# Attention and two FFNs in one kernel: dependent products of a unit further apart, other engines' steps later, M1's block sums moved

## Chip, cores, metric

One core of a Trainium2 chip. The metric is the device time of one execution in microseconds (us). The kernel before takes 1079.6 us, the median of three runs (1079.17 to 1079.61).

## What is computed

```python
qn = q / (norm(q, axis=1) + 1e-6); kn = k / (norm(k, axis=1) + 1e-6)   # norms over the 6016 tokens
a = softmax(kn.T @ qn / tau)                                           # 256 x 256
x = v @ a                                                              # 6016 x 256
h = x @ w_in;  g = h * clip(h + 3, 0, 6) / 6;  x = g @ w_out           # FFN 1: 256 -> 2048 -> 256
h = x @ w_in2; g = max(h, 0) ** 2;             x = g @ w_out2          # FFN 2
```

All inputs are float32; the weights arrive as float64 words.

## The kernel before

**Numbers.** Each float32 matrix is split into a high part `hi` (a cast to fp32r, on ScalarE) and a rest `lo` (the subtraction x - hi). `passes` (lines 298 to 306) makes one product of three TensorE instructions: hi with hi, the left rest with hi, hi with the right rest.

**Stages.** While q and k are loaded, TensorE sums the scores. The softmax is folded into the weights: M1 = a w_in1, in four blocks of 512 columns (blocks 0 to 3, `c4`; line 440 on). The tokens go in six pairs (`WIDTHS`: two column blocks of 512 each, the last pair 448) through layer 1 (j = 0) and then layer 2 (j = 1). The first pair of layer 1 runs as 32 plain steps (lines 834 to 857), because the weights are still being made: a step has `first` (product, relu, multiply, split) and, two steps later, `second`, the products with w_out1. At steps 6, 14 and 22 it makes the next block of M1. Its casts of w_in1 and w_out1 from float64 are spread over the steps by `plan`.

**A Strassen unit.** All other pairs run in units of 256 columns of w_in (`strassen`, lines 702 to 786), eight a pair, 15 places each (`SLOTS`); a place is one product. Seven products make the four blocks of h from sums of blocks of x and of M1. Bank y takes B11, T2, T1 and B22 one on top of the other; ScalarE copies y after the first three as `sa`, `su`, `se`, and the next product into y waits for the copy. Bank x takes B21, bank q takes T3 and later T4. Then h11 = x + sa, h22 = q + se before T4 is added, h21 = q + su after it, and h12 is y itself. T4 waits for the sum h22. Each block goes through relu (ScalarE; layer 1, and h12 in both), multiply (VectorE), `hi` (ScalarE) and `lo` (VectorE) to a group: two products with w_out into `acc`. The eight group products of a unit fill the places that its successor's seven products leave.

**Order.** Every engine works through its instructions in program order. `at(place, go)` notes a step with its place, and `run` emits the steps sorted by place, so the numbers alone set the order on each engine. `PLACE` has the products, `chain` the five steps of each block (add, relu, multiply, hi, lo), `prepare` a pair's input sums and splits (GpSimd makes sums and rests; they start 52.5 places ahead), `times` the nine steps that turn a piece of layer 2's weights into parts while layer 1 runs (the 6th sums on GpSimd, 7th parts on ScalarE, 8th rests on GpSimd, 9th the store).

**M1's sums.** `m1_keep` copies a block of M1 to two buffers, which all blocks share with the operands T1 and T4; `m1_sums` makes four sums on GpSimd; `m1_parts` casts them (ScalarE, 1024 elements) and takes the rest (GpSimd). Only Strassen units use them.

```python
        m1_sum_at = {1: 0}
        m1_sum_at |= {8 * c4 - M1_LEAD + 2: c4 for c4 in range(1, 4)}
...
            if a in m1_sum_at:
                c4 = m1_sum_at[a]
                sums_of[c4] = m1_sums(c4)
            if a - 3 in m1_sum_at:
```

So the sums of blocks 0 to 3 stand at steps 1, 8, 16 and 24, the parts at steps 4, 11, 19 and 27.

## Time and profile before

| | us | |
|---|---|---|
| profiled execution | 1079.58 | its span 1077.8 |
| median of three runs | 1079.6 | 1079.17 to 1079.61 |
| ScalarE busy | 672.5 | 62% of the span |
| GpSimd busy | 256.5 | 24% |
| mean granted TensorE clock | 0.995 | of full speed |

In the rows PE is TensorE, PEld its weight loads, DVE VectorE, ACT ScalarE, POOL GpSimd. A line number is that of the kernel above; a helper's line (L120, the subtraction in `split`) stands for all its callers, so the names tell which. "[1.71 <-ACT wi1h L118]" means: the engine was idle for 1.71 us, and what ended last before it went on was ScalarE's writing of wi1h. PEclk is the granted clock as a share of full speed.

### The profile page before, as it was taken

The numbers are of one execution on the slowest core, as the hardware profiler recorded it, in microseconds if no ns is written. First come the engines' busy times: TensorE is split into PE (matmuls) and PEld (weight loads), VectorE is DVE, ScalarE is ACT, GpSimd is POOL, SyncE is SP. The second block draws the span as 40 slices with busy tenths as digits, with TensorE's granted clock in tenths as the row PEclk, the third lists the DMA queues.
The fourth block names the chain that finished last, engine by engine and source line by source line (L and its number), as shares of the span: only waits on it lengthen the run. The fifth ranks groups of instructions, "written<-read, shape, count | busy, mean of one in ns | idle before, by whom it ended". The sixth has DMA issues, their size and how long they took to land.

```text
span 1077.8 us, 13113 instructions
## 1 busy us (share of the span) xinstructions
PE 1049.4 (97%) x4630; PEld 865.8 (80%) x4630; DVE 866.6 (80%) x1283; ACT 672.5 (62%) x1196; POOL 256.5 (24%) x215
## 2 busy tenths in 40 slices
PE   9989899999989998999999999999999999999998
PEld 8867677877868786788998888888888888888997
DVE  7798977799888888887778878778778778778766
ACT  6677667768767777777767545545445445445443
POOL 0022351154244245234114004104104105004000
PEclk9999999999999999999999999999999999999999
DMA  9721302213212330420344200200200200200100
GB/s 352 301 62 36 98 1 79 93 39 132 93 61 75 110 106 25 143 77 20 127 166 187 102 1 1 78 1 1 79 1 1 79 0 1 74 1 1 40 1 35
DMA packets 25938, 77.66 MB, mean 72 GB/s; under 512 B 2832, under 2 KB 4880, under 8 KB 25872
## 3 DMA queue, kind: packets, MB, share of 16 engines
q1 hardware_dynamic: 25872, 76.82, 19.9%
q8 instruction: 36, 0.59, 0.2%
q14 instruction: 30, 0.25, 0.1%
HBM read 52.95 MB, written 23.86 MB: 71 GB/s over the span
## 4 chain that ended last, share of the span: by engine, by line
PE 75%; DVE 12%; ACT 6%; issue 5%; POOL 2%; DMA 1%; SPq 0%; DVEq 0%; ACTq 0%; POOLq 0%
PE acc L304 13%; PE acc L306 13%; PE acc L305 13%; PE y L304 7%; PE y L306 6%; PE y L305 6%; PE q L304 3%; PE s L294 3%; PE q L306 3%; PE q L305 3%; DVE gs L120 3%; DVE g L744 3%; DVE h L730 2%; PE x L304 2%; PE x L306 2%
## 5 line engine op out<-in xcount | busy, mean ns | idle before, releaser
L120 DVE TENSOR_TENSOR gs<-g,gs 128x512 fp32r<-128x512 f32 (+1 forms) x384 | 280.5, 748 | 65.1 <-ACT gs L753 58.8
L305 PE MATMUL acc<-gs,wo 128*128 128x512 f32 (+1 forms) x768 | 297.0, 387 | 1.1 <-DVE wo L120 1.1
L306 PE MATMUL acc<-gs,wo 128*128 128x512 f32 (+1 forms) x768 | 297.3, 387 | 0.7 <-DVE gs L120 0.7
L304 PE MATMUL acc<-gs,wo 128*128 128x512 f32 (+1 forms) x768 | 297.4, 387 | 0.1
L753 ACT CAST gs<-g 128x512 fp32r<-128x512 f32 (+1 forms) x352 | 214.3, 611 | 116.0 <-DVE g L749 59.3
L306 PEld LDWEIGHTS acc<-gs,wo 128*128 128x128 f32 x768 | 144.7, 188 | 30.6 <-DVE gs L120 3.3
L305 PEld LDWEIGHTS acc<-gs,wo 128*128 128x128 f32 x768 | 144.8, 189 | 28.7 <-DVE wo L120 1.4
L304 PEld LDWEIGHTS acc<-gs,wo 128*128 128x128 f32 x768 | 144.9, 189 | 28.4 <-ACT gs L118 0.8
L685 POOL TENSOR_TENSOR x<-raw,x 128x512 fp32r<-128x512 f32 (+1 forms) x55 | 78.1, 1428 | 324.9 <-ACT x L681 323.7
L749 DVE SCALAR_TENSOR_TENSOR g<-h 128x512 f32<-128x512 f32 (+1 forms) x144 | 123.8, 860 | 3.1
L744 DVE SCALAR_TENSOR_TENSOR g<-r,h 128x512 f32<-128x512 f32 (+1 forms) x120 | 99.8, 832 | 28.7 <-ACT r L736 24.9
L736 ACT ACTIVATE r<-h,three 128x512 f32<-128x512 f32 (+1 forms) x120 | 85.6, 713 | 33.5 <-DVE h L730 32.8
L730 DVE TENSOR_TENSOR h<-q,su 128x512 f32<-128x512 f32 (+1 forms) x88 | 59.6, 677 | 40.2 <-PE q L306 40.0
L730 DVE TENSOR_TENSOR h<-q,se 128x512 f32<-128x512 f32 (+1 forms) x88 | 59.5, 676 | 33.0 <-ACT se L726 32.9
L738 ACT ACTIVATE r<-y 128x512 f32<-128x512 f32 (+1 forms) x48 | 28.3, 590 | 84.4 <-PE y L306 84.4
L726 ACT COPY se<-y 128x512 f32<-128x512 f32 (+1 forms) x88 | 50.6, 575 | 35.2 <-PE y L306 35.1
L726 ACT COPY sa<-y 128x512 f32<-128x512 f32 (+1 forms) x88 | 50.2, 570 | 32.5 <-PE y L306 31.9
L726 ACT COPY su<-y 128x512 f32<-128x512 f32 (+1 forms) x88 | 50.0, 569 | 31.2 <-PE y L306 31.2
L730 DVE TENSOR_TENSOR h<-x,sa 128x512 f32<-128x512 f32 (+1 forms) x88 | 59.4, 675 | 8.4 <-PE x L306 7.3
L670 POOL TENSOR_TENSOR t<-raw 128x512 f32<-128x512 f32 (+1 forms) x11 | 17.2, 1566 | 110.4 <-DMA raw<-x2d 110.4
L294 PE MATMUL s<-qk 128*128 128x256 f32 x188 | 42.5, 386 | 0.6 <-DMA qk<-in_qk 0.6
L294 PEld LDWEIGHTS s<-qk 128*128 128x128 f32 x188 | 36.0, 194 | 6.2 <-DMA qk<-in_qk 1.4
(238 smaller groups left out, 1878.2 us busy)
## 6 DMA issues: line engine op xcount, KB each, us to landing
qk<-in_qk SPq DMA_DIRECT2D x23, 512.0 KB, 7.3
wo<-in_w_out SPq DMA_DIRECT2D x16, 512.0 KB, 4.5
wi<-in_w_in SPq DMA_DIRECT2D x10, 512.0 KB, 4.3
x2d<-o SPq DMA_DIRECT2D x20, 256.0 KB, 2.5
raw<-x2d SPq DMA_DIRECT2D x10, 512.0 KB, 5.3
out<-o SPq DMA_DIRECT2D x20, 256.0 KB, 2.3
raw<-in_vt SPq DMA_DIRECT2D x8, 512.0 KB, 5.8
wo2d<-wo2s SPq DMA_DIRECT2D x8, 512.0 KB, 2.9
```

The costliest lines, as they stand in the source:

```text
L120: (rest or nc.vector).tensor_tensor(out=lo, in0=x, in1=f32(hi), op=ALU.subtract)
L294: nc.tensor.matmul(s_ps[i], lhsT=x[:, C + i * P:C + (i + 1) * P], rhs=x[:, :C], start=(t == 0), stop=(t == NT - 1))
L304: nc.tensor.matmul(ps, lhsT=ah, rhs=bh, start=first, stop=False, skip_group_check=more)
L305: nc.tensor.matmul(ps, lhsT=al, rhs=bh, start=False, stop=False, skip_group_check=more)
L306: nc.tensor.matmul(ps, lhsT=ah, rhs=bl, start=False, stop=last, skip_group_check=more)
L685: nc.gpsimd.tensor_tensor(out=l, in0=ts[r], in1=f32(h), op=ALU.subtract)
L726: nc.scalar.copy(s[tag], s["y"])
L730: nc.vector.tensor_tensor(out=s[which], in0=s[ps], in1=s[tag], op=ALU.add)
L736: nc.scalar.activation(s["r" + which], h, AF.Relu, bias=three)
L744: nc.vector.scalar_tensor_tensor(out=g, in0=s["r" + which], scalar=6.0, in1=h, op0=ALU.min, op1=ALU.mult)
L749: nc.vector.scalar_tensor_tensor(out=g, in0=h, scalar=0.0, in1=r, op0=ALU.max, op1=ALU.mult)
L753: nc.scalar.copy(gs[which][0], s["g" + which])
```

## The change

- Products: `PLACE` puts T2, T3, T1, B22 and T4 at 5, 7, 10, 14 and 16 instead of 4, 6, 8, 12 and 13. T4 now runs at place 1 of the next unit. The groups stand at the other places, as pairs, in the order 11, 22, 12, 21 (before 11, 22, 21, 12).
- The steps of `chain` and the copies su and se stand later.
- M1's sums move to steps 10, 17, 25 and 28, its parts to 14, 20, 27 and 30, each part as two halves. The copies go to a spare tile of each block.
- The parts, rests and store of layer 2's w_in move from 27.4, 28.5 and 36 to 36, 38 and 48.
- The split of the first pair's last step is placed among the first Strassen unit's steps, and the casts of T1 and T4 for the second pair one and two places earlier.

```diff
-PLACE = {0: B11, 2: B21, 4: T2, 6: T3, 8: T1, 12: B22, 13: T4}
+PLACE = {0: B11, 2: B21, 5: T2, 7: T3, 10: T1, 14: B22, 16: T4}
+GROUP = {"11": (3, 4), "22": (6, 8), "12": (9, 11), "21": (12, 13)}
...
-                m32[k] = ops.tile([P, 2 * WMAX], F32, tag=f"op{(T1, T4)[k]}", name=f"m32_{c4}_{k}")[:, :512]
-                nc.scalar.activation(m32[k], mps.pop((c4, k)), AF.Copy, scale=rsum[k])
+                if k == 0:
+                    m32[c4] = spare(2 * c4 + 1, f"m32_{c4}").rearrange("p (k f) -> p k f", k=KC)
+                nc.scalar.activation(m32[c4][:, k, :], mps.pop((c4, k)), AF.Copy, scale=rsum[k])
...
-            hi, lo = (t[:, :, S1:, :] for t in wa1[c4])
-            nc.scalar.copy(hi, st)
-            nc.gpsimd.tensor_tensor(out=lo, in0=st, in1=f32(hi), op=ALU.subtract)
+            for u in range(2):
+                hi, lo = (t[:, u, S1:, :] for t in wa1[c4])
+                nc.scalar.copy(hi, st[:, u, :, :])
+                nc.gpsimd.tensor_tensor(out=lo, in0=st[:, u, :, :], in1=f32(hi), op=ALU.subtract)
...
-            split(*gs, g)
+            if at_step == len(steps) - 1:
+                at(1.6, lambda: split(*gs, g, 0))
+                at(3.0, lambda: split(*gs, g, 1))
+            else:
+                split(*gs, g)
...
-                        after = {T1: -16, T4: -11, T3: 0.3, B22: 3.0}[r]
+                        after = {T1: -17, T4: -13, T3: 0.3, B22: 3.0}[r]
...
-            at(at0 + 5.3, lambda: copy_out("su"))
-            at(at0 + 9.3, lambda: copy_out("se"))
+            at(at0 + 6.3, lambda: copy_out("su"))
+            at(at0 + 11.3, lambda: copy_out("se"))
             chain = {
-                "11": (3.3, 4.6, 6.0, 7.4, 8.9), "22": (10.4, 11.7, 13.1, 14.6, 16.0),
-                "12": (None, 13.4, 15.5, 17.5, 18.8), "21": (14.4, 15.8, 17.3, 19.0, 20.4),
+                "11": (3.6, 7.2, 9.6, 12.2, 13.8), "22": (12.6, 13.9, 15.2, 16.5, 17.8),
+                "12": (None, 15.4, 17.0, 18.5, 20.0), "21": (17.4, 18.8, 20.4, 22.0, 23.4),
             }
...
-                times = (8.7, 9.5, 17.3, 19.4, 22.4, 25, 27.4, 28.5, 36)
+                times = (8.7, 9.5, 17.3, 19.4, 22.4, 25, 36, 38, 48)
...
-        m1_sum_at = {1: 0}
-        m1_sum_at |= {8 * c4 - M1_LEAD + 2: c4 for c4 in range(1, 4)}
+        sums_at, parts_at = {10: 0, 17: 1, 25: 2, 28: 3}, {14: 0, 20: 1, 27: 2, 30: 3}
```

ScalarE in a unit of the second pair, before and after. The names are the block's number, then layer, pair and unit: r11 is relu, gs11 the cast of g11, w32 a piece of layer 2's weights; `0_1_3` is layer 1, pair 1, unit 3.

```order
L736 ACTIVATE r210_1_2_1785<-h210_1_2_1775,three_90 128x512
L726 COPY sa0_1_3_1791<-y0_1_3_1779 128x512
L753 CAST gs120_1_2_1800<-g120_1_2_1783 128x512
L753 CAST gs210_1_2_1808<-g210_1_2_1797 128x512
L736 ACTIVATE r110_1_3_1814<-h110_1_3_1805,three_90 128x512
L726 COPY su0_1_3_1819<-y0_1_3_1779 128x512
L753 CAST gs110_1_3_1831<-g110_1_3_1826 128x512
L224 COPY w32_0_1833<-tawi2_0_1739 128x512
L726 COPY se0_1_3_1842<-y0_1_3_1779 128x512
```

The same part of the program as it is now:

```order
L744 ACTIVATE r120_1_2_1778<-y0_1_2_1675,three_90 128x512
L734 COPY sa0_1_3_1783<-y0_1_3_1772 128x512
L761 CAST gs220_1_2_1785<-g220_1_2_1776 128x512
L761 CAST gs120_1_2_1800<-g120_1_2_1787 128x512
L744 ACTIVATE r210_1_2_1804<-h210_1_2_1794,three_90 128x512
L734 COPY su0_1_3_1819<-y0_1_3_1772 128x512
L761 CAST gs210_1_2_1821<-g210_1_2_1814 128x512
L744 ACTIVATE r110_1_3_1827<-h110_1_3_1802,three_90 128x512
L226 COPY w32_0_1829<-tawi2_0_1736 128x512
L734 COPY se0_1_3_1852<-y0_1_3_1772 128x512
L761 CAST gs110_1_3_1857<-g110_1_3_1838 128x512
```

Before, sa stands behind the relu of block 21, su behind that of block 11, and se behind the cast of block 11. Now sa stands behind the relu of 12, su ahead of the relu of 11, and se ahead of the cast of 11.

GpSimd in the first pair, up to the second pair's first sums, before (st are block sums, wa1 the parts; t, x the second pair's sums and rests):

```order
L484 TENSOR_TENSOR wa1_1l_771<-st1_849,wa1_1h_770 128x2x512
L207 TENSOR_TENSOR st2_1099<-m32_2_0_1034,m32_2_1_1036 128x2x128
L208 TENSOR_TENSOR st2_1099<-st2_1099,m32_2_0_1034 128x2x128
L209 TENSOR_TENSOR st2_1099<-m32_2_0_1034 128x2x128
L210 TENSOR_TENSOR st2_1099<-m32_2_1_1036,st2_1099 128x2x128
L484 TENSOR_TENSOR wa1_2l_1019<-st2_1099,wa1_2h_1018 128x2x512
L670 TENSOR_TENSOR t0_1_0_1244<-raw0_1_0_1159 128x512
L671 TENSOR_TENSOR t0_1_1_1245<-raw0_1_1_1160,t0_1_0_1244 128x512
```

And now, up to the same two sums of the second pair:

```order
L488 TENSOR_TENSOR wa1_0l_531<-st0_895,wa1_0h_530 128x512 x2
L209 TENSOR_TENSOR st1_1120<-m32_1_778 128x2x128
L210 TENSOR_TENSOR st1_1120<-st1_1120,m32_1_778 128x2x128
L211 TENSOR_TENSOR st1_1120<-m32_1_778 128x2x128
L212 TENSOR_TENSOR st1_1120<-m32_1_778,st1_1120 128x2x128
L488 TENSOR_TENSOR wa1_1l_763<-st1_1120,wa1_1h_762 128x512 x2
L678 TENSOR_TENSOR t0_1_0_1238<-raw0_1_0_1151 128x512
L679 TENSOR_TENSOR t0_1_1_1239<-raw0_1_1_1152,t0_1_0_1238 128x512
```

Three blocks are done ahead of the second pair's sums before, and two now; the other two come behind them.

## Rows read from the trace of the kernel before

**Rows 1.** The page, part 1: engine, busy us (share of the span), instructions.

```profile
PE 1049.4 (97%) x4630; PEld 865.8 (80%) x4630; DVE 866.6 (80%) x1283; ACT 672.5 (62%) x1196; POOL 256.5 (24%) x215
```

**Rows 2.** Windows: stretch in us, its length, then busy us (instructions) by engine, clock, DMA.

```profile
core 0: us, PE busy (x) PEld busy (x) DVE busy (x) ACT busy (x) POOL busy (x), PEclk, DMA share, GB/s
50.40:175.00 124.60, 112.67 (x463) 85.24 (x463) 105.07 (x165) 88.90 (x153) 40.45 (x31) 0.99 0.16 52
175.00:455.00 280.00, 269.33 (x1145) 214.47 (x1144) 239.08 (x344) 209.21 (x373) 96.84 (x89) 0.99 0.24 85
600.00:1000.00 400.00, 400.00 (x1762) 330.20 (x1762) 314.53 (x439) 201.44 (x356) 79.42 (x55) 1.00 0.07 24
```

**Rows 3.** TensorE's waits, whole span: line, what ended them, us in total, times, longest.

```profile
PE mp L304 <- ACT wi1h L118: 6.6, 3, 3.5
PE y L304 <- ACT su L726: 5.8, 8, 2.6
PE y L304 <- ACT se L726: 2.5, 3, 0.9
PE q L304 <- DVE h L730: 2.2, 2, 1.9
PE y L304 <- ACT sa L726: 1.3, 3, 0.8
PE mp L306 <- DVE wi1l L120: 1.2, 1, 1.2
...
PE acc L305 <- DVE wo L120: 1.1, 1, 1.1
```

**Rows 4.** Windows, columns as in rows 2: three stretches of layer 1.

```profile
320.60:331.00 10.40, 8.81 (x32) 7.11 (x33) 8.08 (x10) 7.49 (x14) 6.42 (x5) 0.84 0.38 139
140.00:160.00 20.00, 20.00 (x88) 16.17 (x87) 14.81 (x20) 13.32 (x23) 13.46 (x10) 1.00 0.00 1
128.00:140.00 12.00, 8.49 (x30) 6.34 (x29) 10.92 (x14) 6.86 (x13) 5.52 (x3) 0.86 0.00 0
```

**Rows 5.** Line 120, VectorE's subtractions: times, then ns min/median/max.

```profile
L120 DVE TENSOR_TENSOR gs<-g,gs x384: 609/684/1789, 60.9 to 1071.1; 128x512 fp32r<-128x512 f32 x160, 128x448 fp32r<-128x448 f32 x32
...
L120 DVE TENSOR_TENSOR wo<-tawo,wo x8: 684/693/1206, 62.0 to 151.3; 128x512 fp32r<-128x512 f32 x8
```

**Rows 6.** Timeline around M1 block 1: start, length in us, engine, line ... [idle before it].

```profile
74.72 1.03 ACT L483 CAST wa_0h<-st 128x1024 fp32r<-128x1024 f32 x1
...
75.83 2.37 POOL L484 TENSOR_TENSOR wa_0l<-st,wa_0h 128x1024 fp32r<-128x1024 f32 x1 [13.15 <-ACT wa_0h L483]
...
76.89 0.50 PE L304 MATMUL mp<-wi1h,eth 128*128 128x512 f32 x1 [1.71 <-ACT wi1h L118]
76.97 1.77 DVE L120 TENSOR_TENSOR wi1l<-tawi,wi1h 128x512 fp32r<-128x512 f32 x1
...
78.80 0.50 PE L306 MATMUL mp<-wi1l,eth 128*128 128x512 f32 x1 [1.17 <-DVE wi1l L120]
```

**Rows 7.** Timeline around M1 block 3.

```profile
128.97 1.82 DVE L157 SCALAR_TENSOR_TENSOR tawi<-tbwi,tawi 128x512 int32<-128x512 int32 x1
...
132.40 1.74 DVE L162 CUSTOM_DVE_ANT_0 tawi<-tawi,tywi 128x1024 uint16<-128x1024 uint16 x1
...
134.84 0.55 PE L304 MATMUL mp<-wi1h,eth 128*128 128x512 f32 x1 [3.51 <-ACT wi1h L118]
```

**Rows 8.** Timeline, a unit of the second pair.

```profile
222.06 1.78 DVE L744 SCALAR_TENSOR_TENSOR g<-r,h 128x512 f32<-128x512 f32 x1
...
223.87 0.62 ACT L753 CAST gs<-g 128x512 fp32r<-128x512 f32 x1 [3.31 <-DVE g L744]
...
225.03 0.50 PE L304 MATMUL y<-x,wa_2h 128*128 128x512 f32 x1 [0.92 <-ACT se L726]
```

**Rows 9.** Timeline, a unit of the third pair.

```profile
319.90 0.62 ACT L235 CAST wa2s<-w 128x512 fp32r<-128x512 f32 x1 [1.47 <-POOL w L210]
...
322.19 0.50 PE L304 MATMUL y<-x,wa_3h 128*128 128x512 f32 x1 [2.57 <-ACT su L726]
```

More of the change, by code (lines that the diff above doesn't have):

```diff
@@ L470, in m1_keep @@
             for k in range(KC):
-                m32[k] = ops.tile([P, 2 * WMAX], F32, tag=f"op{(T1, T4)[k]}", name=f"m32_{c4}_{k}")[:, :512]
-                nc.scalar.activation(m32[k], mps.pop((c4, k)), AF.Copy, scale=rsum[k])
+                if k == 0:
+                    m32[c4] = spare(2 * c4 + 1, f"m32_{c4}").rearrange("p (k f) -> p k f", k=KC)
+                nc.scalar.activation(m32[c4][:, k, :], mps.pop((c4, k)), AF.Copy, scale=rsum[k])
         def m1_sums(c4):
             st = spare(2 * c4, f"st{c4}").rearrange("p (u a c) -> p u a c", u=2, a=4)
-            m = [m32[k].rearrange("p (u f c) -> p u f c", u=2, f=2) for k in range(KC)]
+            m = [m32[c4][:, k, :].rearrange("p (u f c) -> p u f c", u=2, f=2) for k in range(KC)]
             combine(st, [[t[:, :, f, :] for f in range(2)] for t in m], lambda t, i: t[:, :, i, :], nc.gpsimd)
@@ L601, in product, with first @@
                 passes(hs[at], [(weight0(f, k), x0[k, n])], k == 0, k == KC - 1)
-        def first(at, between):
-            n, f = steps[at]
-            h = hs.pop(at)
+        def first(at_step, between):
+            n, f = steps[at_step]
+            h = hs.pop(at_step)
             r = tmp("r", w0, f"r0_{n}_{f}")
@@ L774, in strassen @@
                     at(at0 + place_, lambda go=go, which=which: go(which))
-            free = [x for x in range(SLOTS) if x not in PLACE]
-            blocks = [(which, d) for which in ("11", "22", "21", "12") for d in range(KC)]
-            for x, (which, d) in zip(free, blocks):
+            for which, places in GROUP.items():
                 f, n = int(which[0]) - 1, int(which[1]) - 1
-                first_, last = u == 0 and which in ("11", "22"), u == NU - 1 and which in ("12", "21")
-                at(at0 + SLOTS + x, lambda which=which, f=f, n=n, d=d, first_=first_, last=last: group(
-                    j, p, u, f, n, d, gs[which], first_, last
-                ))
-                if last:
-                    engine = nc.scalar if (d + n) % 2 == 0 else nc.vector
-                    at(at0 + SLOTS + x + 1.4, lambda n=n, d=d, engine=engine: evict(j, p, n, d, engine))
+                first_, last = u == 0 and which in ("11", "22"), u == NU - 1 and which in ("21", "12")
+                for d, x in enumerate(places):
+                    at(at0 + SLOTS + x, lambda which=which, f=f, n=n, d=d, a=first_, z=last: group(
+                        j, p, u, f, n, d, gs[which], a, z
+                    ))
+                    if last:
+                        engine = nc.scalar if (d + n) % 2 == 0 else nc.vector
+                        at(at0 + SLOTS + x + 1.4, lambda n=n, d=d, engine=engine: evict(j, p, n, d, engine))
         unit_at = {}
@@ L849, in attention_then_two_ffns @@
             issue()
-            if a in m1_sum_at:
-                c4 = m1_sum_at[a]
-                sums_of[c4] = m1_sums(c4)
-            if a - 3 in m1_sum_at:
-                c4 = m1_sum_at[a - 3]
-                m1_parts(c4, sums_of.pop(c4))
+            if a in sums_at:
+                sums_of[sums_at[a]] = m1_sums(sums_at[a])
+            if a in parts_at:
+                m1_parts(parts_at[a], sums_of.pop(parts_at[a]))
             run(-(len(steps) - 1 - a) * SLOTS / 4)
-        free = [x for x in range(SLOTS) if x not in PLACE]
+        free = sorted(set(range(SLOTS)) - {x % SLOTS for x in PLACE})
         for x, go in zip(free, [(n, f, d, gs) for n, f, gs in pending for d in range(KC)]):
```

## Prediction

> **What bounds the kernel now.** Read the page's shares first: TensorE is busy for 97% of the span, VectorE for 80% [rows 1]. That says TensorE is the bound, but not whether it runs at its pace, since its records overlap. So count its products by stretch [rows 2]. From 600 to 1000 us, in the second layer, 1762 products start in 400 us, one per 0.227 us, and no engine makes it wait. That is the pace of a 512-column product. From 50.4 to 175 us (the first pair of layer 1 and the hand-over to the second) 463 products would need 105.1 us at that pace and take 124.6: 19.5 us lost. From 175 to 455 us (the other pairs of layer 1, but for the last) 1145 would need 259.9 and take 280: 20.1 us lost. So about 40 us can be won, all in layer 1. The three products of one place take 3 x 0.227 = 0.68 us.
>
> The list of TensorE's waits [rows 3] says who ends them: M1's products wait for w_in1's parts (6.6 and 1.2 us), one group for w_out1 (1.1), and the Strassen products for the copies su, se, sa and the sum h (5.8, 2.5, 1.3, 2.2). These sum to 20.7 us. The lost time is larger by 19: TensorE's records overlap, so that a wait shows shorter than it is and the shortest do not show, and after the longest waits the granted clock falls. The 10.4 us from 320.6 show 0.84 and the 12 us from 128 show 0.86 [rows 4]; with the levels 2.4 and 1.2 GHz that is about 1.7 us lost each.
>
> Next, why the waits happen. A VectorE subtraction with both inputs in SBUF takes 0.68 us in the median and up to 1.79 [rows 5]; the long ones, here and in other operations of that kind 1.74 to 1.82 us [rows 6 to 8], lie beside a GpSimd operation. ScalarE works in its program's order, so a cast that waits for VectorE holds the copy behind it. Before 225.03 a multiply took 1.78 us, the cast of g11 had ScalarE idle for 3.31 us until it was done, and the copy se, for which TensorE waited, comes behind that cast in ScalarE's order [rows 8]. At 322.19 the head of ScalarE's queue was the cast of layer 2's weights, waiting 1.47 us for GpSimd; su came behind it and TensorE waited 2.57 us [rows 9].
>
> **The change, part by part.** *M1's sums and parts.* They leave steps 1 to 11 of the first pair. (1) The sums of step 1 ran beside the split of w_out1, whose rest took 1.21 us instead of 0.69 [rows 5]; the subtraction in front of it was stretched alike, 1.0 us in all, and TensorE waited 1.1 there [rows 3]: -1.1. (2) The parts of step 4 put a 1.03 us cast in front of w_in1's cast, and their 2.37 us subtraction stretched w_in1's rest to 1.77 us [rows 6]: 1.03 + 1.08 = 2.1 of the two waits of 1.71 and 1.17: -2.1. (3) The third M1 wait of [rows 3] is 6.6 - 1.71 - 3.51 = 1.4 us, behind the same cast and subtraction at step 11: -1.4. (4) At 134.84 TensorE waits 3.51 us and runs on at half clock for a while. Three stretched VectorE operations precede it (the first and the last are shown), 1.8 - 0.7 = 1.1 us too long each [rows 7]. GpSimd's preparation of the next pair, the cause of the last two, stays where it is, and now the parts of block 1 stand at step 20 in place of block 2's at 19. I keep two of the three stretches and let one (1.1), the cast's share (0.6) and the fall of the clock (1.7) go: -3.4, between 0 (the move from 19 to 20 changes nothing) and -5.2. First pair: -8.0, with ends of -4 (only the waits of steps 1 and 4, the nearest rows) and -12.
>
> The cover for the moved steps is the first pair's second half: 140 to 160 us ran without a lost product, with GpSimd busy 13.5 of 20 us and VectorE 14.8 [rows 4]. One block's parts (2.37 us [rows 6]) and one block's four sums, which I put at as much again, come in: 4.7 of the 6.5 us that GpSimd has free there. The hand-over to the second pair, behind it, I leave as it is. The four casts that become eight (0.62 us for 512 elements [rows 8], 1.03 for 1024 [rows 6]) cost ScalarE 0.2 us a block, beside products.
>
> *Places in a unit.* T2 stands 4 places after its predecessor's end instead of 3, T1 too, T4 5 after T1's end instead of 4: 0.68 us more for sa, su and the sum h22. T1 to B22 stays at 3. In ScalarE's order su now stands ahead of relu11 and se ahead of the cast of g11, on which the wait of [rows 8] rested; the weights' parts come 8.6 places later, after GpSimd has finished the sums, which takes the 1.47 us of [rows 9] away. Of the waits in [rows 3], the seven others for su make 3.2 us, 0.46 each, and none for sa is over 0.8, so 0.68 us more cover most of each; the 2.57 one goes by 1.47 + 0.68 and the order, with its clock. The longest wait for h, 1.9 us, keeps 1.2. That leaves about 2 us of the 20.1.
>
> What is late next? The rests lo, which the groups wait for. Their distance falls from 7 to 4 places (g11), 4 to 3.2 (g22), 7 to 4 (g12), and stays at 3.6 (g21). For g22 that is 3.2 x 0.68 = 2.2 us, plus 0.45 because only a group's third product reads lo, less its own 0.69: 1.9 us. One stretched operation is 1.1 us late, two are 2.2. Each of four pair boundaries has two GpSimd stretches of the kind of [rows 8]; I put one 0.7 us wait on each and double it for what I have not seen: 5.7 us. So the Strassen stretch keeps 7.7 of 20.1: -12.4, with ends of -4.3 (only the wait of [rows 9] and its clock: 2.57 + 1.7) and -20.
>
> *The rest.* Layer 2 loses nothing now [rows 2] and has no relu for three of four blocks: 0, between 0 and +3 (one 0.5 us wait in each of six pairs). At the end T4 runs behind the last unit's fifteen places, but the first unit has one product less: 0, bounds one product, 0.7 us each way. DMA: weight stores and the two loads of a pair move by up to 12 places on SyncE's queue, far ahead of their use: 0.
>
> Sum: -8.0 - 12.4 = -20.4. The profiled execution took 1079.58 us, the median of the runs is 1079.6, so it stands for them: **1059.2 us**. A measurement of this kernel tells about 0.2% (2.2 us) from no change.
>
> **A rule against it.** The rows show met operations lasting 1.1 us longer [rows 7]. The Trainium skill (SBUF — State Buffer, "Who interferes with whom") says that a VectorE operation with two SBUF inputs and a GpSimd operation that reads SBUF share a port pair as an exclusive lock, so the second "fully blocks". By that the moved sums block VectorE as long at their new steps, and nothing is won in the first pair: 1067.2. The trace agrees with the blocking; whether cover is there is the rival below.
>
> **The rivals.**
> - *VectorE is the real bound of layer 1 (0.14).* Its 239.1 us in the Strassen stretch [rows 2] would be 92% of 259.9 us. Then waits for su return as waits for lo, and only the wait of [rows 9] goes: 1079.6 - 8.0 - 4.3 = 1067.3. Against: 8% is left, and units differ.
> - *The moved sums are paid back (0.12).* GpSimd, at 13.5 of 20 us before, gets behind; the rests of T3 and B22, its last ones, come late and the groups wait for stretched rests. All 8.0 return: 1079.6 - 12.4 = 1067.2. For: T3's rest now stands behind the parts of block 3. Against: rests have 2 steps of cover.
> - *Almost all goes (0.12).* No new wait for lo, half of the first pair's loss left: 1079.6 - 14 - 18 = 1047.6.
> - *No change (0.05).* Copies are late because VectorE is, and it stays as late: both gains fail, 1079 +- 2.
> - *Slower (0.07).* Group g22 waits in every unit. It decides where its rest starts over 1.9 us late in a quiet unit; at 2.6 us late, each of 40 layer-1 units pays 0.7 us: 28 us against the 20.4 won, 1087. For: the closest distance of the new table. Against: quiet units have 1.5 us of VectorE time free (85% of 10.2 us busy).
>
> **How the numbers follow.** The forecast has 0.50; its own range is 1052 to 1066, from the ends of its terms. Faster: 0.50 + 0.14 + 0.12 + 0.12 = 0.88. Same 0.05, slower 0.07. The range 1047 to 1073 takes in the three faster rivals and the partial loss of both gains; it leaves out the last two cases and a few hundredths of tails.
>
> **What would show it.** Right: products from 50.4 us on at nearly 4.4 per us; waits for su and sa under 2 us in sum; no wait of a y product over 1 us; a granted clock of 1.0 where [rows 9] lie; waits of acc for gs of a few us in their place; the first M1 wait near 1 us. Wrong: waits of acc for gs over 15 us (VectorE as the bound), or a wait for T3's parts at the hand-over (the sums paid back), or any wait in layer 2.

## The result, and the profile after

The changed kernel takes 1067.9 us in the median (1067.63 to 1068.54), the kernel before in the same measurement 1079.4 (1077.63 to 1079.61): the ratio is 0.9898, with a 95% interval of 0.9881 to 0.9915. It is faster by about 11.5 us. The forecast was 1059.2: the sign is right, the range of 1047 to 1073 holds the result, and the gain is a little over half of what was put. The forecast's own range, 1052 to 1066, does not hold it: the measured time lies at the 1067.2 and 1067.3 of the two rivals in which one of the two gains fails; below, each holds in part and neither alone.

In what follows, lines of the changed kernel stand 2 to 8 lower than those of before (L120 is L122 now, L726 is L734, L730 is L738, L744 is L752). The page's first part shows TensorE's share one point up, and VectorE's too, because the span is shorter:

```profile
PE 1044.1 (98%) x4630; PEld 864.1 (81%) x4630; DVE 858.6 (81%) x1283; ACT 662.9 (62%) x1200; POOL 256.1 (24%) x219
```

The same three windows as in [rows 2], now of the changed kernel:

```profile
50.40:175.00 124.60, 115.75 (x474) 86.08 (x474) 106.70 (x169) 92.17 (x162) 43.19 (x35) 1.00 0.18 56
175.00:455.00 280.00, 274.03 (x1183) 220.95 (x1182) 245.45 (x353) 212.77 (x381) 96.46 (x89) 0.99 0.26 90
600.00:1000.00 400.00, 400.00 (x1772) 332.17 (x1771) 310.46 (x443) 197.78 (x359) 75.93 (x53) 1.00 0.07 24
```

In the 280 us of the Strassen stretch 1183 products start, not 1145. At 0.227 us each they need 268.5 us, so 11.5 us are still lost there, of 20.1. In the first 124.6 us 474 need 107.6, so 17.0 are lost, of 19.5. TensorE's waits, whole span:

```profile
PE acc L308 <- DVE gs L122: 6.2, 10, 2.5
PE mp L306 <- ACT wi1h L120: 2.5, 2, 1.4
...
PE acc L307 <- DVE wo L122: 1.1, 1, 1.1
PE q L306 <- DVE h L738: 0.9, 1, 0.9
...
PE y L306 <- ACT se L734: 0.7, 1, 0.7
```

Against [rows 3]: the waits for su and sa are gone, that for se is 0.7 us where it was 2.5, and in their place groups wait 6.2 us for the rests of g. The 1.1 us for w_out1 are there as before.

**How the traces are compared below.** In the fourteen profiles of this study the first product of M1 starts between 49.6 and 53.1 us, though no kernel moves an instruction ahead of it. So this table counts from that product on: to the first product of unit 0 (the first pair), on to that of unit 40 (the Strassen stretch of layer 1), on to that of unit 80 (layer 2 but for its last pair), and from there to the end. Units count from 0; eight make a pair of tokens, and unit 14 is the "fourteenth unit" of the expectations. All times are differences of start times in us, each from one trace, and the granted clock falls to half for a few microseconds in one profile and not in another of the same instructions. So a single unit can differ by 1.6 us from chance: unit 14 took 14.7 us before, with the fall of [rows 4], and 13.1 in experiment 2, which runs the same program there and shows no fall; unit 22 took 15.3 us in the changed kernel, with a fall, and 13.8 in experiment 5, again the same program there, without one. Differences of 1 to 2 us between the sums below decide nothing by themselves.

| kernel | first pair | units 0 to 39 | units 40 to 79 | tail | sum |
|---|---|---|---|---|---|
| before | 115.1 | 421.1 | 408.6 | 82.9 | 1027.8 |
| changed | 111.7 | 412.3 | 407.5 | 83.8 | 1015.4 |
| 1 units only | 114.2 | 411.8 | 407.6 | 83.8 | 1017.4 |
| 2 M1 only | 111.7 | 420.7 | 408.6 | 82.9 | 1024.0 |
| 3 later parts only | 115.1 | 423.4 | 408.6 | 82.9 | 1030.0 |
| 4 order only | 115.1 | 413.5 | 407.6 | 82.9 | 1019.0 |
| 5 sums held | 112.4 | 410.7 | 407.5 | 83.8 | 1014.5 |
| 6 order undone | 111.8 | 445.8 | 414.5 | 83.8 | 1055.9 |
| 7 order and M1 | 111.7 | 413.1 | 407.6 | 82.9 | 1015.3 |
| 8 conversion later | 111.7 | 411.7 | 407.4 | 83.8 | 1014.7 |
| 9 parts early | 111.7 | 413.6 | 407.5 | 83.8 | 1016.7 |
| 10 three edits, parts early | 111.7 | 411.3 | 407.6 | 84.2 | 1014.8 |
| 11 three edits, parts late | 111.8 | 411.2 | 407.6 | 84.2 | 1014.7 |
| 12 order, M1, two edits | 111.7 | 410.8 | 407.6 | 82.9 | 1013.0 |

And single units, from first product to first product:

| unit | before | changed | 1 | 3 | 4 | 6 | 7 | 8 | 9 | 12 |
|---|---|---|---|---|---|---|---|---|---|---|
| 5 | 11.6 | 10.3 | 10.2 | 12.4 | 10.2 | 13.0 | 10.2 | 10.3 | 10.2 | 10.2 |
| 12 | 11.6 | 10.3 | 10.2 | 12.4 | 10.2 | 12.9 | 10.2 | 10.3 | 10.2 | 10.2 |
| 14 | 14.7 | 10.4 | 11.4 | 10.6 | 14.4 | 11.4 | 14.7 | 10.4 | 11.4 | 10.5 |
| 15 | 10.2 | 11.2 | 11.6 | 11.6 | 10.2 | 12.7 | 10.2 | 11.2 | 11.6 | 12.2 |
| 22 | 15.4 | 15.3 | 14.3 | 15.0 | 14.7 | 14.7 | 14.4 | 11.7 | 13.6 | 12.0 |

A unit without a wait takes 10.2 us (45 products of 0.227). So the change took 3.4 us from the first pair, 8.8 from units 0 to 39, 1.1 from layer 2, and cost 0.9 in the tail.

### The profile page after: what moved, and what is told of

It reads as the page before. It is cut to its first block, busy times and chain, and to the rows that moved or that the text cites. A ratio compares the mean times of both kernels' runs of the same rounds, so it can differ in the third digit from the quotient of the medians.

```text
span 1065.9 us, 13054 instructions
## 1 busy us (share of the span) xinstructions
PE 1044.1 (98%) x4630; PEld 864.1 (81%) x4630; DVE 858.6 (81%) x1283; ACT 662.9 (62%) x1200; POOL 256.1 (24%) x219
## 4 chain that ended last, share of the span: by engine, by line
PE 72%; DVE 14%; ACT 7%; issue 3%; POOL 3%; DMA 1%; SPq 0%; ACTq 0%; POOLq 0%
PE acc L308 13%; PE acc L307 12%; PE acc L306 12%; PE y L306 6%; PE y L307 6%; PE y L308 6%; DVE gs L122 5%; PE s L296 3%; PE q L308 3%; PE q L306 3%; PE q L307 3%; DVE g L752 3%; PE x L308 1%; PE x L306 1%; PE x L307 1%
## 5 line engine op out<-in xcount | busy, mean ns | idle before, releaser
L122 DVE TENSOR_TENSOR gs<-g,gs 128x512 fp32r<-128x512 f32 (+1 forms) x384 | 296.8, 773 | 72.7 <-ACT gs L761 65.0
L761 ACT CAST gs<-g 128x512 fp32r<-128x512 f32 (+1 forms) x352 | 209.1, 613 | 65.2 <-DVE g L752 46.1
L757 DVE SCALAR_TENSOR_TENSOR g<-h 128x512 f32<-128x512 f32 (+1 forms) x144 | 117.0, 813 | 0.0
L734 ACT COPY se<-y 128x512 f32<-128x512 f32 (+1 forms) x88 | 50.6, 575 | 105.3 <-PE y L308 105.3
L738 DVE TENSOR_TENSOR h<-q,se 128x512 f32<-128x512 f32 (+1 forms) x88 | 59.5, 676 | 64.1 <-ACT se L734 63.9
L734 ACT COPY su<-y 128x512 f32<-128x512 f32 (+1 forms) x88 | 50.7, 576 | 90.8 <-PE y L308 79.2
L752 DVE SCALAR_TENSOR_TENSOR g<-r,h 128x512 f32<-128x512 f32 (+1 forms) x120 | 97.4, 812 | 6.0 <-ACT r L744 5.6
L744 ACT ACTIVATE r<-h,three 128x512 f32<-128x512 f32 (+1 forms) x120 | 85.5, 713 | 8.6 <-DVE h L738 8.1
L738 DVE TENSOR_TENSOR h<-q,su 128x512 f32<-128x512 f32 (+1 forms) x88 | 59.2, 672 | 1.2
L738 DVE TENSOR_TENSOR h<-x,sa 128x512 f32<-128x512 f32 (+1 forms) x88 | 58.9, 670 | 0.0
L734 ACT COPY sa<-y 128x512 f32<-128x512 f32 (+1 forms) x88 | 50.7, 576 | 5.8 <-PE y L308 0.4
L757 DVE SCALAR_TENSOR_TENSOR g<-y,r 128x512 f32<-128x512 f32 (+1 forms) x48 | 32.5, 677 | 19.9 <-ACT r L746 19.7
```

The lines of the kernel that those rows point to most:

```text
L122: (rest or nc.vector).tensor_tensor(out=lo, in0=x, in1=f32(hi), op=ALU.subtract)
L734: nc.scalar.copy(s[tag], s["y"])
L738: nc.vector.tensor_tensor(out=s[which], in0=s[ps], in1=s[tag], op=ALU.add)
L744: nc.scalar.activation(s["r" + which], h, AF.Relu, bias=three)
L752: nc.vector.scalar_tensor_tensor(out=g, in0=s["r" + which], scalar=6.0, in1=h, op0=ALU.min, op1=ALU.mult)
L757: nc.vector.scalar_tensor_tensor(out=g, in0=h, scalar=0.0, in1=r, op0=ALU.max, op1=ALU.mult)
```

## The experiments

Theory A: the gain is the sum of its parts, of which the distances of the products and the later parts of the weights carry the Strassen stretch. Theory B: VectorE, beside GpSimd, bounds the units around a pair's start, and waits only change their names. Theory C: what counts is ScalarE's order, su and se ahead of the steps that wait for VectorE.

### The change in pieces: experiments 1 to 4

**1, units only**, an edit of the changed kernel:

```diff
-                times = (8.7, 9.5, 17.3, 19.4, 22.4, 25, 36, 38, 48)
+                times = (8.7, 9.5, 17.3, 19.4, 22.4, 25, 27.4, 28.5, 36)
-        sums_at, parts_at = {10: 0, 17: 1, 25: 2, 28: 3}, {14: 0, 20: 1, 27: 2, 30: 3}
+        sums_at, parts_at = {1: 0, 8: 1, 16: 2, 24: 3}, {4: 0, 11: 1, 19: 2, 27: 3}
```

> The changed kernel with the sums and the parts of M1 put back to their old steps (sums 1, 8, 16, 24; parts three steps later) and the old places for the weights' parts; so of the change it keeps the new places of a unit's products and steps, and the cast of a block by halves. Theory A (the pieces add up): by the two traces the Strassen stretch ended 8.8 us sooner from its first unit to its last, layer 2 1.1 us and the first pair 3.4 us; one unit, the fourteenth, alone gave 4.3 us, and it is the one in which the weights' parts stood in ScalarE's way. The units alone should then give 8.8 - 4.3 + 1.1 = 5.6 us: 1073.8 us, waits on su and sa gone, the fourteenth unit still near 14.7 us. Theory B (VectorE beside GpSimd bounds the units at a pair's boundary, whatever the order of the products): the waits come back under other names, at most 2 us gained, 1077 to 1079 us.

Measured: 1070.1 us beside 1080.3 for the kernel before, ratio 0.9904 (0.989 to 0.9918). Both theories miss: by its trace 10.4 us are won, nearly the change's whole 12.4. Unit 14 falls to 11.4 us without the later parts.

**2, M1 only**, an edit of the kernel before: the diff's M1 part (copies to spare tiles, casts by halves, `sums_at` and `parts_at`) and nothing else.

> The kernel before with the M1 part of the change alone (sums at steps 10, 17, 25, 28, parts at 14, 20, 27, 30, the cast by halves). Theory A: the two traces differ by 3.4 us over the first pair and its first unit takes up 0.4 us, so 1079.4 - 3.4 = 1076.0 us; the wait of 3.5 us ahead of the third block's products is near 1.4 us, the one of 1.1 us behind the first block stays, since GpSimd starts the first block's sums within 0.5 us of where it did. Theory B (what the sums no longer delay in the middle, they delay at the end of the first pair, where the first unit of the Strassen stretch waits for them): 1078.5 to 1079.5 us.

Measured: 1077.1 us, ratio 0.9975 (0.9966 to 0.9985): about 2.7 us, 3.8 by the trace. Theory A's 3.4 us fits the first pair (115.1 to 111.7). But the second pair, units 0 to 7, takes 86.0 us where it took 85.0, all of it in unit 0 (10.6 for 9.6): some is paid back there, as B says, though not all. The other 1.4 us of the 3.8 are chance: unit 14 without its fall of the clock, and unit 22, which differs by 0.9 us with the same program.

**3, later parts only**, an edit of the kernel before:

```diff
-                times = (8.7, 9.5, 17.3, 19.4, 22.4, 25, 27.4, 28.5, 36)
+                times = (8.7, 9.5, 17.3, 19.4, 22.4, 25, 36, 38, 48)
```

> The kernel before with the last three weights' parts of a pair at 36, 38 and 48 places rather than 27.4, 28.5 and 36, and nothing else. Theory A: the fourteenth unit, where ScalarE stands behind a GpSimd part of the weights, gives its 4.3 us back by this alone: 1075.1 us, and the other units within 0.3 us of the kernel before. Theory B (the units' gain hangs on the distance of the products; with the products where they were, ScalarE's later work does not reach TensorE sooner): at most 1 us, 1078.4 us or more.

Measured: 1084.8 us, ratio 1.0042 (1.003 to 1.0054): slower. Unit 14 gives 4.1 us back as A said, but units 4, 5, 11, 12, 15, 16, 29 and 30 take 0.4 to 1.4 us longer each, and the sum is 2.2 us against it by the trace. Its waits show which grew: there are six for h now and four for sa, where [rows 3] have two and three. Which step stands ahead of each was not followed further.

```profile
PE q L304 <- DVE h L730: 4.2, 6, 1.9
PE y L304 <- ACT su L726: 3.5, 7, 0.8
PE y L304 <- ACT sa L726: 2.7, 4, 1.2
```

**4, order only**, an edit of the kernel before. Every product stays; on ScalarE su (5.3) now comes ahead of relu of h11, se (9.3) ahead of the cast of g11:

```diff
-                "11": (3.3, 4.6, 6.0, 7.4, 8.9), "22": (10.4, 11.7, 13.1, 14.6, 16.0),
+                "11": (3.3, 5.4, 7.2, 9.4, 10.6), "22": (10.4, 11.7, 13.1, 14.6, 16.0),
```

> The kernel before with only the order of the steps of h11 on the other engines changed: su is copied out ahead of relu of h11, se ahead of the cast of g11; every product stands where it stood. Theory C (the waits on su and se, 8.3 us in the trace of the kernel before, come from ScalarE's order alone and not from the distance of the products): 4 to 6 us gained, 1073.5 to 1075.5 us, with waits on su and se gone. Theory A (the distance counts: what su no longer waits for, h11 and g11 wait for, and the products behind them stand as near as before): no more than 2 us either way, 1077.5 to 1081.5 us, with the waits on su replaced by waits of the products of g11.

Measured: 1072.2 us, ratio 0.9929 (0.9916 to 0.9942). Theory C holds, with more than the 4 to 6 us that it named: 7.7 us by the measurement, 8.8 by the trace from the first M1 product on. The edit also changes VectorE's order in one place: the sum h22 now comes ahead of the rest of g11. TensorE's waits for h stay (2.6 us, 2.2 before), so the gain is not seen there; experiment 6 changes ScalarE's order alone. Its waits for the copies:

```profile
PE y L304 <- ACT sa L726: 3.3, 4, 1.3
PE q L304 <- DVE h L730: 2.6, 2, 2.1
PE y L304 <- ACT su L726: 2.5, 1, 2.5
...
PE y L304 <- ACT se L726: 0.7, 1, 0.7
```

The eight waits for su are one, that of unit 14. ScalarE in the unit of [rows 8] reads like this in the trace of experiment 4:

```profile
223.28 0.59 ACT L726 COPY se<-y 128x512 f32<-128x512 f32 x1 [1.51 <-PE y L306]
224.91 0.62 ACT L753 CAST gs<-g 128x512 fp32r<-128x512 f32 x1 [1.04 <-DVE g L744]
```

In [rows 8] the cast stood first, waited 3.31 us for VectorE, and se began 0.53 us behind it, just ahead of the waiting product. Now se starts as soon as TensorE has filled y, and the cast waits where nobody waits for it.

### The order undone in the changed kernel: experiment 6

```diff
-            at(at0 + 6.3, lambda: copy_out("su"))
-            at(at0 + 11.3, lambda: copy_out("se"))
+            at(at0 + 7.3, lambda: copy_out("su"))
+            at(at0 + 12.3, lambda: copy_out("se"))
```

> The changed kernel, with su copied out one place later (behind relu of h11 on ScalarE) and se one place later (behind the cast of g11), so that the order of these steps on ScalarE is that of the kernel before, while the products keep their new places. Theory A (the distance of the products is what takes the waits away): at most 1 us slower, 1068 to 1069 us. Theory C (ScalarE's order is): su and se wait again behind VectorE's work, waits of y on su and on se of 4 to 8 us are back, 1072 to 1076 us.

Measured: 1111.4 us, ratio 1.0286 (1.0269 to 1.0304). Theory C has the sign and missed the size by far; A is out. Moving su by one place puts it behind two steps: the cast of the last unit's g21 (7.0) and relu of h11 (7.2). Its waits, and one of them:

```profile
PE y L306 <- ACT su L734: 31.4, 30, 2.5
PE y L306 <- ACT se L734: 3.0, 4, 1.8
```

```profile
469.95 0.68 DVE L752 SCALAR_TENSOR_TENSOR g<-r,h 128x512 f32<-128x512 f32 x1
470.66 0.62 ACT L761 CAST gs<-g 128x512 fp32r<-128x512 f32 x1 [1.93 <-DVE g L752]
471.19 0.72 ACT L744 ACTIVATE r<-h,three 128x512 f32<-128x512 f32 x1
...
471.81 0.56 ACT L734 COPY su<-y 128x512 f32<-128x512 f32 x1
...
472.43 0.50 PE L306 MATMUL y<-x,wa_1h 128*128 128x512 f32 x1 [1.33 <-ACT su L734]
```

The last product into y had started at 467.99. ScalarE was idle for 1.93 us at the cast's place in its queue, did the cast and the relu, and only then the copy, so TensorE waited. Why is this worse than the kernel before, which had the same order? There T4 stood ten places ahead of the next T1 (13 and 8 + 15); now it stands nine ahead (16 and 10 + 15). The chain T4, h21, relu, multiply, cast g21, relu 11, su, T1 has to pass in that distance, once a unit. So the new places of the products are longer for sa and h22 and shorter for this chain, and su's place ahead of the cast keeps it off TensorE's path. This reason is read from the places; no run gave T4 its ten places back.

### Do the distances add anything: experiments 7 and 9

**7, order and M1**: the edit of 4 and the M1 part of 2, on the kernel before.

> The kernel before with the order of su and se on ScalarE (which alone took 8.8 us off the time behind the first M1 product, by its trace) and the M1 part of the change (3.8 us by its trace); products, weights' parts and tail as before. If the two are worth the same together as apart, 12.6 us behind the first M1 product: about 1067 us, the changed kernel's time without its new distances of products; if the new distances are worth something of their own, or the M1 part is paid back at the first unit, 2 us or more slower than the changed kernel, 1070 us.

Measured: 1069.2 us, ratio 0.9904 (0.9889 to 0.9918). From the first M1 product on 1015.3 us, the changed kernel 1015.4: the two parts add up (8.8 + 3.8 = 12.6, found 12.5; by the measured ratios 7.7 + 2.7 = 10.4, found 10.4). What the changed kernel has beyond them, distances and later parts, is 0.7 us better in units 0 to 39, no more than chance, and 0.9 worse in the tail, which every trace with the new places shows. The intervals of the two ratios, 0.9904 and 0.9898, overlap almost wholly.

**9, parts early**: the changed kernel with the old `times` of the diff in 1.

> The changed kernel with the old places of the weights' parts (27.4, 28.5 and 36 in place of 36, 38 and 48), and nothing else. By the third experiment the late places took 4.1 us off the fourteenth unit and gave 6 us back in others, with the products near; with the products apart the first experiment, which had the early places, ended its Strassen stretch of layer 1 in 411.8 us from its first unit, the changed kernel in 412.3. Theory 1 (the late parts are worth nothing or less once ScalarE's order is right): 1066.5 to 1068 us, the fourteenth unit near 11.4 us in place of 10.4, units 8, 22 and 29 some 0.5 to 1 us shorter each. Theory 2 (they carry the 4.3 us of the fourteenth unit, as the prediction had it): 1070 to 1072 us, the fourteenth unit near 14.7.

Measured: 1068.2 us, ratio 0.9884 (0.987 to 0.9899). Theory 2 is out: unit 14 takes 11.4 us, not 14.7. By the trace the early places cost 1.3 us, by the ratio they gain as much; so the later parts are worth less than can be told apart. They move time between units: 14, 18 and 25 are shorter with them, 8 and 29 longer.

### The sums of block 0: experiment 5

In the changed kernel the wait for w_out1 did not move, because the sums did not: their place in the program is later, but GpSimd's queue is in order and empty, so they start at once. The trace of the changed kernel:

```profile
58.82 1.18 POOL L209 TENSOR_TENSOR st<-m 128x256 f32<-128x256 f32 x1 [49.25 <-PE h L308]
...
61.29 1.23 DVE L122 TENSOR_TENSOR gs<-g,gs 128x512 fp32r<-128x512 f32 x1
...
63.71 0.50 PE L307 MATMUL acc<-gs,wo 128*128 128x512 f32 x1 [1.07 <-DVE wo L122]
```

So GpSimd was given something to wait for:

```diff
+            if a == 10:
+                nc.gpsimd.tensor_tensor(out=small(1), in0=f32(gs[1])[:, 0:1], in1=f32(gs[1])[:, 0:1], op=ALU.subtract)
             if a in sums_at:
```

> The changed kernel, and one GpSimd subtraction of one column put ahead of the sums of M1's first block, which reads the rest of the gated block of step 10 and so cannot start before it: now the sums really start late, where in the changed kernel they started at 58.82 us, as before. Theory A (the first term of the prediction was right in its mechanism and failed only since the sums did not move): VectorE is not stretched around 60 us, the wait of 1.07 us on wo at 63.71 us is gone, nothing comes in its place, 1.1 us less from the first M1 product to the end. Theory B (the sums stretch VectorE as long wherever they stand): the wait goes, and about as much comes back around 83 us, where VectorE copies the second block of M1: 0 (-0.3 to +0.3).

Measured: 1067.7 us, ratio 0.9889 (0.9876 to 0.9903). The trace of experiment 5 around both places:

```profile
62.33 0.69 DVE L122 TENSOR_TENSOR wo<-tawo,wo 128x512 fp32r<-128x512 f32 x1
...
63.08 0.50 PE L307 MATMUL acc<-gs,wo 128*128 128x512 f32 x1 [0.22 <-DVE wo L122]
...
95.29 0.74 POOL L209 TENSOR_TENSOR st<-m 128x256 f32<-128x256 f32 x1
...
97.73 0.96 DVE L155 TENSOR_SCALAR tawi<-raw13l 128x512 int32<-128x512 int32 x1
98.61 0.95 DVE L156 TENSOR_SCALAR tbwi<-tbwi 128x512 f32<-128x512 f32 x1
...
102.85 0.50 PE L306 MATMUL mp<-wi1h,eth 128*128 128x512 f32 x1 [0.55 <-ACT wi1h L120]
```

The mechanism of the prediction's term (1) was right: with the sums away, the rest of w_out1 takes 0.69 us again and TensorE waits 0.22, and the stretch up to M1's block 1 is 1.0 us shorter. But the sums stretch VectorE's conversion of w_in1 where they now stand (0.96 and 0.95 us instead of 0.42), and M1's block 2 waits for it: from block 2 to block 3 it takes 1.65 us longer. The first pair is 0.7 us longer in all. Theory B, with its place 20 us later than it was expected. (That the sum of this trace is lower than the changed kernel's comes from unit 22.)

### What is left: experiments 8, 10, 11 and 12

Unit 22 kept its 15.3 us. The trace of the changed kernel shows why:

```profile
399.54 1.75 POOL L684 TENSOR_TENSOR raw<-raw,raw 128x512 f32<-128x512 f32 x1
400.05 1.78 DVE L159 SCALAR_TENSOR_TENSOR tawo<-tbwo,tawo 128x512 int32<-128x512 int32 x1
...
401.86 1.63 DVE L164 CUSTOM_DVE_ANT_0 tawo<-tawo,tywo 128x1024 uint16<-128x1024 uint16 x1
403.42 0.68 DVE L122 TENSOR_TENSOR gs<-g,gs 128x512 fp32r<-128x512 f32 x1
...
404.16 0.79 PE L308 MATMUL acc<-gs,wo 128*128 128x512 f32 x1 [2.46 <-DVE gs L122]
```

Ahead of the rest of g21 VectorE has two steps of a conversion, both stretched to more than twice their 0.68 us beside GpSimd's sums. TensorE waits 2.46 us, and the window behind shows the granted clock at 0.79:

```profile
402.00:410.00 8.00, 5.84 (x19) 4.69 (x20) 6.64 (x9) 4.84 (x9) 2.58 (x2) 0.79 0.16 66
```

**8, conversion later**, an edit of the changed kernel:

```diff
                     times = (8.7, 9.5, 17.3, 19.4, 22.4, 30)
+                    if u == 5:
+                        times = [x + 12 for x in times]
```

> The changed kernel with the conversion of one piece of layer 2's weights (the sixth of the second kind, on VectorE L155 to L164) placed 12 places later, behind the fourth pair's preparation. Theory: unit 22 still takes 15.3 us because VectorE runs that conversion (two operations, 1.78 and 1.63 us, both stretched beside GpSimd's sums for the pair) ahead of the rest of g21, for which TensorE waits 2.46 us and then runs some 2 us at the lower clock; moved, unit 22 is near 11 us, 1063.5 us. Rival (VectorE has no room around a pair's start, wherever the conversion stands): a wait of the same length comes one or two units later, 1067 to 1068 us.

Measured: 1067.2 us, ratio 0.9884 (0.9871 to 0.9898). Unit 22 falls by 3.6 us, as the theory says; units 23, 24 and 29 take 0.6, 1.3 and 1.0 longer, as the rival says. Two waits of its trace stand where the moved steps now meet a pair's preparation:

```profile
422.85 0.50 PE L308 MATMUL acc<-gs,wo 128*128 128x512 f32 x1 [1.29 <-DVE gs L122]
...
475.67 0.50 PE L308 MATMUL acc<-gs,wo 128*128 128x512 f32 x1 [1.21 <-DVE gs L122]
```

Net gain by the trace: 0.7 us. Beside experiment 5, whose unit 22 took 13.8 us with the changed kernel's program, it is none: units 0 to 39 take 411.7 us here and 410.7 there. So the rival holds.

**10 and 11, three edits**: the long steps of that conversion 5.7 places later, the parts of M1's block 1 at step 18, and the last unit of all with the places and chain of the kernel before (su ahead of relu). 10 has the early parts of the weights, 11 the late ones.

```diff
+                    times = (8.7, 9.5, 23, 24.5, 27.5, 34) if u == 5 else (8.7, 9.5, 17.3, 19.4, 22.4, 30)
...
-        sums_at, parts_at = {10: 0, 17: 1, 25: 2, 28: 3}, {14: 0, 20: 1, 27: 2, 30: 3}
+        sums_at, parts_at = {10: 0, 17: 1, 25: 2, 28: 3}, {14: 0, 18: 1, 27: 2, 30: 3}
...
+LAST_PLACE = {0: B11, 2: B21, 4: T2, 6: T3, 8: T1, 12: B22, 13: T4}
+LAST_GROUP = {"11": (1, 3), "22": (5, 7), "21": (9, 10), "12": (11, 14)}
```

> The changed kernel with the early places of the weights' parts and three more edits: the last unit of all has the places and the chain of the kernel before (with su ahead of relu of h11), the parts of M1's second block stand at step 18 rather than 20, ahead of the sums for the second pair, and the conversion of the sixth piece of layer 2's second weights stands 5.7 places later in its two long steps. Expected from the traces: the tail gives its 0.9 us back, the copies of M1's last block no longer wait (1.6 us of waits between 131 and 139 us), unit 22 loses 2 to 4 of its 15.3 us, of which the eighth experiment says that up to two thirds come back: 3 to 4 us less than the changed kernel, 1064 us. If VectorE has no room there, 1066 us.

> The same three edits on the changed kernel with its own late places of the weights' parts: 1064.5 us, within 0.5 us of the tenth if the places of the weights' parts are worth nothing, 3 us under it if they carry the fourteenth unit.

Measured: 1067.9 us, ratio 0.9885 (0.9869 to 0.9902), and 1066.7, ratio 0.9875 (0.9858 to 0.9891). The expected 3 to 4 us did not come. The tail got 0.4 us longer, not 0.9 shorter: what follows the last product takes 4.05 us again, as before the change, where the changed kernel takes 4.4, but that product starts 0.8 us later. A likely reason is that the last unit's old places meet the new ones of the unit ahead of it; it was not shown. The parts of block 1 at step 18 removed the waits between 136 and 139 us and put others of 1.4 us at 127.9 and 1.7 at 132.9, in the trace of 10; the first pair stayed at 111.7. In 11 unit 22 fell by 3.7 us, and units 23, 24 and 29 took 2.5 us longer.

**12, order, M1 and two edits**, on the kernel of 7:

```diff
+                    times = (8.7, 9.5, 23, 24.5, 27.5, 34) if u == 5 else (8.7, 9.5, 17.3, 19.4, 22.4, 30)
+                elif u == 3:
+                    times = (8.7, 9.5, 17.3, 19.4, 22.4, 25, 30, 33.5, 42)
```

> The seventh experiment (the kernel before with su and se ahead on ScalarE and the M1 part of the change: products near, weights' parts early, old tail) with two edits for the two units that were still long in it: the parts of the fourth piece of layer 2's first weights stand at 30, 33.5 and 42 rather than 27.4, 28.5 and 36, and the two long steps of the sixth piece of the second weights 5.7 places later. Theory (what is left in those units is one step in ScalarE's way and one in VectorE's, and the distance of the products is worth nothing): unit 14 falls from 14.65 to about 11 us, unit 22 from 14.36 to about 11.5, 1 to 2 us come back in the units behind them; 1010 to 1012 us from the first M1 product to the end, where the seventh had 1015.3 and the changed kernel 1015.4; 1064 to 1066 us in all. If near products leave VectorE and GpSimd no room for the moved steps: 1014 us or more from the first M1 product to the end, 1068 us.

Measured: 1066.0 us (1065.47 to 1067.1), ratio 0.9879 (0.9862 to 0.9895). By the trace 1013.0 us from the first M1 product on, between the theory's 1010 to 1012 and the other case's 1014. That is 2.4 less than the changed kernel, of which some 1.4 are the fall of the clock in the changed kernel's unit 22, for there is none in this trace's units; by the ratios it is the same or better. Units 14 and 22 fall to 10.5 and 12.0, and units 15, 23 and 24 take 3.7 us more than in 7. What is left are waits for sa, again a copy behind a cast that waits for VectorE:

```profile
322.79 0.62 ACT L755 CAST gs<-g 128x512 fp32r<-128x512 f32 x1 [2.36 <-DVE g L746]
...
324.08 0.56 ACT L728 COPY sa<-y 128x512 f32<-128x512 f32 x1
```

To put sa ahead of that cast as well was not tried.

## Why the prediction was right, and where it was not

**Faster: right, from the cause it named second.** The prediction gave the waits for su two reasons, 0.68 us more distance for each and the order on ScalarE for se and for the one of [rows 9]. Experiment 4 takes the distance away and keeps the order: seven of the eight waits for su are gone. Experiment 6 keeps the distance and takes the order away: thirty waits. So the step "0.68 us more cover most of each" failed as a reason, though the waits it spoke of did go. The distance was read from copy to product alone; the copy's start, which the queue ahead of it sets, was what varied.

**First pair: -8.0 put, -3.4 measured.** Term (1), -1.1, gave 0: the sums of step 1 did not move in time, since nothing stood ahead of them on GpSimd; what moves an instruction is a wait ahead of it, not its number. Term (2), -2.1, gave 1.8: of 1.71 + 1.17 us [rows 6] one wait of 1.1 is left. Term (3), -1.4, gave 1.1: that wait is gone. Term (4), -3.4, gave 0.4. Its wait of 3.51 us [rows 7] fell to 1.38 and 0.30 and the clock stayed at 1.00, as put. But GpSimd did the parts of block 1 there and the second pair's sums behind them, and VectorE was stretched again and again:

```profile
127.64 2.97 POOL L488 TENSOR_TENSOR wa_1l<-st,wa_1h 128x512 fp32r<-128x512 f32 x2 [11.71 <-ACT wa_1h L487]
127.69 1.79 DVE L164 CUSTOM_DVE_ANT_0 tawi<-tawi,tywi 128x1024 uint16<-128x1024 uint16 x1
...
130.19 0.50 PE L306 MATMUL mp<-wi1h,eth 128*128 128x512 f32 x1 [1.38 <-ACT wi1h L120]
...
130.57 1.74 POOL L678 TENSOR_TENSOR t<-raw 128x512 f32<-128x512 f32 x1
...
131.09 1.78 DVE L122 TENSOR_TENSOR gs<-g,gs 128x512 fp32r<-128x512 f32 x1
...
132.39 1.62 POOL L679 TENSOR_TENSOR t<-raw,t 128x512 f32<-128x512 f32 x1
132.79 1.52 DVE L155 TENSOR_SCALAR tawo<-wo 128x512 int32<-128x512 int32 x1
...
135.27 0.62 ACT L120 CAST gs<-g 128x512 fp32r<-128x512 f32 x1 [2.83 <-DVE g L613]
...
135.79 0.47 ACT L466 ACTIVATE wa_3h<-mp,rs 128x256 fp32r<-128x256 f32 x1
...
136.31 0.49 PE L306 MATMUL h<-x,wa_3h 128*128 128x512 f32 x1 [0.45 <-ACT wa_3h L466]
```

Four waits follow from 136.31 to 138.93, 1.3 us together, for copies of M1's last block that came late; against 0.227 us a product they and the products just behind them lose 2.7 us. The first copy (135.79) stands in ScalarE's queue behind a cast that waited 2.83 us for VectorE (135.27): the same queue that held se in [rows 8]. The prediction priced the wait and did not ask what the same VectorE work was late for next. Nor were the 1.7 us of the clock to be won here. In experiment 2 the same stretch, from M1's last block to unit 0, shows the clock at 0.95, and takes as long as in the changed kernel at 1.00:

```profile
130.66:164.84 34.18, 31.51 (x121) 22.96 (x120) 26.94 (x34) 21.85 (x39) 24.76 (x20) 0.95 0.00 0
127.97:162.15 34.18, 30.60 (x122) 21.74 (x120) 26.94 (x34) 21.83 (x39) 24.79 (x20) 1.00 0.00 0
```

With the clock halved TensorE reaches M1's last block later and waits there for less; VectorE's 26.94 us of work are the same in both. The clock at 1.00 was luck, too: of the eight profiles with the M1 part at the changed kernel's steps four show a fall there.

**The rule weighed against it.** What was moved stretched VectorE at its new place in the two traces looked at: 0.96 for 0.42 us beside block 0's sums in experiment 5, 1.79 for 0.68 beside block 1's parts at 127.69 above. The Trainium skill (SBUF — State Buffer, "Who interferes with whom") has the second of two such operations fully blocked; as the prediction applied it, nothing is won by moving them. The trace agrees for block 0 (experiment 5: 1.0 us won, 1.65 lost) and mostly for term (4), 0.4 of 3.4; for terms (2) and (3) there was cover, and 2.9 us were won. The sum by that rule, 1067.2, comes close to the result, but not for its reason alone: of the gain that did not come, 4.6 us are the first pair's and 3.6 the Strassen stretch's.

**The rival "moved sums are paid back"** holds in part: with the M1 part, units 0 to 7 take 1.0 us longer (experiment 2 against before) or 0.9 (7 against 4), over a quarter of the first pair's gain of 3.4 and 3.3. With the new places of the products it is 1.8 us (9 against 1) of a gain of 2.5, all of it in unit 0 (9.5 for 7.8): there most of what the M1 part wins is paid back. The sign that the prediction named for this, a wait for T3's parts at the hand-over, is in the changed kernel's trace, though small:

```profile
168.31 0.50 PE L308 MATMUL q<-x,wa_0h 128*128 128x512 f32 x1 [0.18 <-POOL x L693]
```

**Strassen stretch: -12.4 put, -8.8 measured.** The old waits were to keep 2 us and keep 0.9, that for h (the 0.7 for se is an old one of unit 0). The new waits for the rests lo were put at 5.7 us; the list has 6.2, of which 0.5 are the first pair's and 5.7 the units', so their sum was right. The size that was missed is what a wait costs beyond itself: the prediction doubled 2.8 us of waits to 5.7 lost, but unit 22 alone loses 5.1 us of the 11.5 (15.3 - 10.2) for waits of 0.41 and 2.46, behind the second of which the clock falls. Of these 5.1 us 1.4 are chance, since experiment 5 loses 3.6 there without the fall. Before the change the unit lost as much for three waits (sa 0.8, su 0.5, h 1.9), which went; those for lo came in their place, and the unit gained 0.1 us. The rival "VectorE is the real bound" is right for such units alone: experiments 8, 11 and 12 show that one step moved out gives 2 to 4 us there and that half or more of it comes back in the next units.

**[rows 9]: 4.3 us, right in size (unit 14 gives 4.3), though its causes do not add.** Each of two was nearly enough alone. Experiment 3 shows that the later parts do it by themselves (4.1), at 6 us elsewhere; experiment 1 shows that the new places do 3.3 of it without them, at 1.9 us in units 15 and 16; the order alone gives 0.3 (experiment 4). The clock's part was luck: without the fall unit 14 takes 13.1 us with nothing changed in it (experiment 2), so some 1.6 of the 4.3 us come and go.

**Layer 2: 0 put, -1.1 measured.** In most pairs of layer 2 one unit had taken a quarter of a microsecond too long; that went with the order alone (experiment 4). **Tail: 0 put, +0.9**, outside the bound of 0.7: the last product starts 0.5 us later and what follows it takes 0.4 longer. T4 and the groups' last products and evictions stand later in the last unit; which of them costs it was not told apart; experiments 10 and 11 took back what follows the last product and not its start. **Slower, g22 late in every unit:** no unit without a pair's preparation shows it; those take 10.2 us.

## What to carry to other kernels

A wait for a copy need not be a matter of the distance between producer and consumer; here it was one of what waits ahead of the copy in its own engine's queue: read the engine's idle time just ahead of it, and move the copy ahead of the step that waits for a third engine. A later place in an in-order queue moves work only if something ahead of it waits; where nothing does, the instruction starts as before. When two engines stretch each other, moving one of them moves the stretch, and something is won only where the work at the new place has slack (terms 2 and 3 had it, block 0's sums did not), so name the work that will be late there before counting the gain.
